# Two fp32 transformer layers on one core: the MLP's first norm between output projections, the last projection quarter inside the MLP, pinned row maxima, earlier V weights, another QKV order

## The chip, the cores and the metric

The kernel runs on one core of one Trainium2 chip. Its time is the device time of one execution in microseconds (us); three runs were shown before the change. The profile is one execution recorded by the hardware profiler. Engines are called as the profile calls them: PE is TensorE (matmuls), DVE is VectorE, ACT is ScalarE, POOL is GpSimd, and SP issues DMAs. ACT and POOL issue DMAs too.

## The reference

Two layers, with the same weights in both, on x of shape (1, 2048, 512) in fp32:

```python
def _A_ref(x, wqkv, wo):
    B, S, D = x.shape
    H = 32
    Dh = D // H
    qkv = (lambda x, *d: x.transpose(*d))((x @ wqkv).reshape(B, S, 3, H, Dh), 2, 0, 3, 1, 4)
    q, k, v = qkv[0], qkv[1], qkv[2]
    scores = jnp.einsum("bhqd,bhkd->bhqk", q, k) * (Dh ** -0.5)
    p = _softmax(scores, axis=-1)
    o = jnp.einsum("bhqk,bhkd->bhqd", p, v)
    return (lambda x, *d: x.transpose(*d))(o, 0, 2, 1, 3).reshape(B, S, D) @ wo

def _B_ref(x, w1, b1, w2):
    h = jnp.einsum("bsd,df->bsf", x, w1) + b1
    sp = jnp.log1p(jnp.exp(-jnp.abs(h))) + jnp.where(h > 0, h, jnp.zeros_like(h))
    act = h * jnp.tanh(sp)
    return jnp.einsum("bsf,fd->bsd", act, w2)

x = x + _A_ref(_layernorm(x, axis=-1), A_wqkv, A_wo)
x = x + _B_ref(_layernorm(x, axis=-1), B_w1, B_b1, B_w2)
# and both lines once more
```

D is 512, there are 32 heads of 16, 2,048 positions, and the MLP is 1,792 wide.

## The kernel before

**Number format.** A value x that a projection multiplies is kept as two parts, hi = x rounded by a copy to the matmul's format and lo = x - hi. `mm3` (L158) multiplies hi by hi, hi by lo and lo by hi: three matmuls of 128x512 for one product. `split_psum` (L154) makes the two parts of a result: ACT copies hi, DVE subtracts lo. In names, `th`/`tl`, `oh`/`ol`, `ah`/`al` are such pairs.

**Tiles.** The positions are worked in four chunks of 512 (`c`). Large tiles (8 KB a partition) come from one pool `blk` of 22 buffers; `tmp` holds small ones: `raw` (three buffers, shared by the blocks `pt` on their way to memory and by weights before they are split), `f` (two, shared by the activation `hb`, the normalised rows `xn` and the attention output `ot`), `he` and `hr` (one each, shared with the reciprocals `den`). The matmul results live in banks `s` (three), `mx` (two pairs) and `acc` (one).

**Norm.** `norm_parts` (L165) takes the statistics of four row blocks (L176, L177), the inverse root on POOL (L173), scales (`xn`, L188), transposes on PE (`tp`, L196) and splits (L197). It is a generator: every `yield` is a place where a caller goes on with something else.

**QKV.** `qkv` goes through a written list `order` of pairs (m, c): m is a block of 128 columns (0 to 3 queries, 4 to 7 keys), c the chunk. Each takes 12 matmuls, is split into `pt` and stored to memory (`scr`) on ACT's DMA queue (L466). When all chunks of m = 0 and m = 4 are through, `prep_qk(0)` (L236) loads the rows of the first four heads back, and the blocks that follow have some row maxima between them (`some_max`, L289 on PE and L293 on DVE). The V weights `rqkv4`, `rqkv5` are fetched after (5, 3) on ACT's DMA queue and split at once by ACT (L114) and POOL (L115). In layer 0 the split weights are stored (`keep`, L103) and in layer 1 read back (`ready`). The norm of the last chunk in layer 1 (`late`) is called when the list first asks for that chunk.

**Attention.** `run` makes 512 steps per layer of scores (L343, L353), exponentials on ACT (L344, L354) and the product with V (`pv`, L369), and beside them the maxima of the blocks 24 steps ahead. A block's maxima become the negative rows `nf` (ACT, L315) and `np` (POOL, L316 and L317), which SP's DMAs put into the query rows. Work is hung on steps by `hooks`. PE's order is chained by `pe` (L225).

**Output.** `HeadsOut` (L512) loads a chunk's sums and denominators (`num`, `den`), inverts (L529), spreads the reciprocals through memory (`rscr` L531, `rec` L537, both on POOL's queue), multiplies (L541) and splits (L545 to L548). The four numbers at L688 say at which steps from the end this is done for chunks 0 to 2; chunk 3 is done after the loop. `wo_parts` (L551) is the projection of a chunk, 48 matmuls, with the residual added on DVE (L567). Projection 0 fills the end of the attention loop, then come projection 1, the whole norm of chunk 0 for the MLP (L712), projection 2, projection 3.

**MLP.** `hid` (L572) makes one 128-wide step `f` of 14: 12 matmuls, then a chain over ACT (L582, L584, L586, L587), DVE (L583, L585, L590, L592) and POOL (L588, L591) to `ah` and `al`. `outp` (L595) multiplies them into four banks, two steps later (`LAG`). The norms of the next chunks are hung on steps with `spread` (L204).

**Order.** A scheduler orders the instructions of each engine by a simulated time line, except where `tc.keep_in_program_order` pins one to its written place.

Of the kernel before, what the change touches and what calls it, by code (L numbers as in the profile page):

```python
# [18 lines left out]
P = 128  # L19
# [22 lines left out]
FILL = 13  # L42
# [4 lines left out]
MAX_M = (2, 6, 3, 7)  # L47
# [5 lines left out]
def kernel(ctx: ExitStack, tc: tile.TileContext, x, wqkv, wo, w1, b1, w2, out):  # L53
# [45 lines left out]
    kept = {}  # L99
# [5 lines left out]
    def split_load(key, src, a, b, later=None, behind=False):  # L105
        t = b8([P, 2, a, b], F32R, "s" + key)
        raw = tmp.tile([P, a, b], F32, tag="raw", name="r" + key, bufs=3)
        if behind:
            tc.keep_in_program_order(nc.scalar.dma_start(raw, src))
        else:  # L110
            nc.sync.dma_start(raw, src)

        def split():
            nc.scalar.activation(t[:, 0], raw, AF.Copy)  # L114
# [25 lines left out]
    def ready(key, l, behind=False):  # L140
        t = b8(list(kept[key].shape), F32R, f"{key}l{l}")
        if behind:
            tc.keep_in_program_order(nc.scalar.dma_start(t.bitcast(F32), kept[key].bitcast(F32)))
        else:
            nc.sync.dma_start(t.bitcast(F32), kept[key].bitcast(F32))
        return t
# [7 lines left out]
    def split_psum(hi, lo, src):  # L154
        nc.scalar.activation(hi, src, AF.Copy)  # L155
        nc.vector.tensor_tensor(lo, src, hi.bitcast(F32), op=ALU.subtract)
# [8 lines left out]
    def norm_parts(src, nm, got, key, tag, fine=False):  # L165
        st = tmp.tile([P, NCH, 6], F32, tag="st", name=f"st{nm}")
        mv = tmp.tile([P, NCH, 2], F32, tag="mv", name=f"mv{nm}")
        ve = tmp.tile([P, NCH], F32, tag="ve", name=f"ve{nm}")
        rs = tmp.tile([P, NCH], F32, tag="rs", name=f"rs{nm}")

        def rstd(t, n):
            nc.vector.tensor_scalar(ve[:, t : t + n], mv[:, t : t + n, 1], EPS, None, op0=ALU.add)
            nc.gpsimd.tensor_tensor(rs[:, t : t + n], ve[:, t : t + n], mhalf[:, t : t + n], op=ALU.pow)  # L173

        for t in range(NCH):
            nc.vector.bn_stats(st[:, t], src[:, t])  # L176
            nc.vector.bn_aggr(mv[:, t], st[:, t])  # L177
            if fine:
                rstd(t, 1)
        if not fine:  # L180
            rstd(0, NCH)
        yield
        th = b8([P, KT, CW], F32R, f"th{nm}")
        tl = b8([P, KT, CW], F32R, f"tl{nm}")
        got[key] = (th, tl)
        for t in range(NCH):
            xn = t512("f", f"xn{nm}{t}")
            nc.vector.tensor_scalar(  # L188
                xn, src[:, t], mv[:, t, 0:1], rs[:, t : t + 1], op0=ALU.subtract, op1=ALU.mult
            )  # L190
            if tag == "mx":
                tp = ps.tile([P, 2, 512], F32, tag=tag, name=f"tp{nm}{t}")[:, 0]
            else:
                tp = pbank(tag, f"tp{nm}{t}")
            for k in range(KT):
                nc.tensor.transpose(tp[:, ts(k, P)], xn[:, ts(k, P)], ident)  # L196
            split_psum(th[:, :, ts(t, P)], tl[:, :, ts(t, P)], tp.rearrange("p (k n) -> p k n", k=KT))  # L197
            yield
# [5 lines left out]
    def spread(hooks, at, src, nm, got, key):  # L204
        parts = norm_parts(src, nm, got, key, "acc")
        for c, f in at:
            hooks.setdefault((c, f), []).append(lambda: next(parts, None))

    class Attention:
# [26 lines left out]
        def prep_qk(self, g):  # L236
            l = self.l
            ks, qs = [], []
            for u in range(HG // 2):
                k = b8([P, S], F32R, f"ks{l}{g}{u}")  # L240
                q = b8([P, S], F32R, f"qs{l}{g}{u}")
                m, h0 = divmod(g * HG + 2 * u, P // DH)
                for e in range(2):
                    r0 = e * HALF
                    nc.sync.dma_start(
                        k[r0 + KROWS : r0 + MROWS].bitcast(F32).rearrange("p (r n) -> p r n", n=P),
                        ones[:, None, :].to_broadcast([MROWS - KROWS, S // P, P]),
                    )
                    yield
                    for t, parts, base in ((k, K_PARTS, NCH), (q, Q_PARTS, 0)):  # L250
                        for j, a in enumerate(parts):
                            nc.sync.dma_start(
                                t[r0 + j * DH : r0 + (j + 1) * DH].bitcast(F32),
                                self.scr[base + m][a, (h0 + e) * DH : (h0 + e + 1) * DH, :].bitcast(F32),
                            )
# [51 lines left out]
        def max_rows(self, b, nm):  # L307
# [8 lines left out]
            nc.gpsimd.tensor_copy(np_[:, 0], nf)  # L316
            nc.gpsimd.tensor_tensor(np_[:, 1], nf, np_[:, 0].bitcast(F32), op=ALU.subtract)  # L317
# [111 lines left out]
    def load_qkv(l, wts, which, behind=False, later=None):  # L429
        for j in which:  # L430
            key = f"qkv{j}"
            if l:
                wts[j] = ready(key, l, behind)
            elif j < 4:
                wts[j] = split_load(key, *cols(wqkv, j), behind=behind, later=later)
            else:
                wts[j] = split_load(key, *rows2(wqkv[:, 2 * D : 3 * D], j - 4), behind=behind)

    def qkv(l, wts, tt, order, late):
# [4 lines left out]
        def some_max():  # L444
            if ahead[0] < AHEAD + PRE:
                att.chained = True
# [6 lines left out]
        for m, c in order:  # L453
# [15 lines left out]
            if (m, c) == (5, 3) and 4 not in wts:  # L469
                load_qkv(l, wts, (4, 5), behind=True)  # L470
            if m in (0, 4):
                done += 1
                if done == 2 * NCH:
                    for _ in att.prep_qk(0):
                        pass
            elif done == 2 * NCH and m in MAX_M:
                some_max()
        for c in range(NCH - 1):
            for i, _ in enumerate(v_parts(l, c, wts, tt, att, False)):
                if i % KT == KT - 1:  # L480
# [31 lines left out]
    class HeadsOut:  # L512
# [15 lines left out]
        def invert(self):  # L528
            tc.keep_in_program_order(nc.vector.reciprocal(self.den, self.den))  # L529
            for q in range(NCH):  # L530
                nc.gpsimd.dma_start(self.rscr[:, ts(q, P)], self.den[ts(q, H)])  # L531

        def spread(self):
            self.rec = b8([P, KT, CW], F32, f"rec{self.l}{self.c}")
            rows = self.rscr.rearrange("(k h) n -> k h n", k=KT)
            for h in range(P // DH):
                nc.gpsimd.dma_start(self.rec[ts(h, DH)], rows[:, h][None].to_broadcast([DH, KT, CW]))  # L537

        def parts(self, aside):
            nm = f"{self.l}{self.c}"  # L540
            tc.keep_in_program_order(nc.vector.tensor_tensor(self.num, self.num, self.rec, op=ALU.mult))  # L541
# [6 lines left out]
            nc.vector.tensor_tensor(ol, self.num, oh.bitcast(F32), op=ALU.subtract)  # L548
            self.out = oh, ol

    def wo_parts(l, c, outs, wot, x2, pe):  # L551
        oh, ol = outs[c].out
        for t in range(NCH):
            if t % 2 == 0:
                acc = ps.tile([P, 2, 512], F32, tag="mx", name=f"wo{l}{c}{t}")
            for k in range(KT):
                mm3(
                    acc[:, t % 2],
# [6 lines left out]
            if t % 2:  # L565
                x2v = x2[:, t - 1 : t + 1]
                nc.vector.tensor_tensor(x2v, acc, x2v, op=ALU.add)  # L567
# [68 lines left out]
    splits = []  # L636
    xc = [load_x(0)]
    load_qkv(0, wts, (0, 2), later=splits)
    xc.append(load_x(1))
    for c in range(NCH):  # L640
        parts = norm_parts(xc[c], f"q0{c}", tt, c, "mx", c == 0)
        next(parts)
        if c == 0:
            for split in splits:
                split()
        for _ in parts:
            pass
        if c == 0:
            load_qkv(0, wts, (1, 3))
        if c + 2 < NCH:  # L650
            xc.append(load_x(c + 2))
    for l in range(2):
        if l == 0:
# [4 lines left out]
        att = qkv(l, wts, tt, order, late)  # L658
# [29 lines left out]
        for c, (t0, t1, t2, t3) in enumerate(((-42, -23, -21, -18), (-26, -22, -20, -13), (-10, -6, -4, 0))):  # L688
# [14 lines left out]
        for i in range(1, 3):  # L703
            load_w1(i)
            load_w2(i - 1)
        for _ in fill:
            pass
        for i, _ in enumerate(project(1)):
            if i == 2 * KT:
                outs[3].invert()  # L710
                outs[3].spread()
        norm(x2s[0], f"m{l}0", tts, 0, "acc")  # L712
        for i, _ in enumerate(project(2)):
            if i == 2 * KT:
                outs[3].parts(False)
        for _ in project(3):
            pass
        for i in range(3, 7):
            load_w1(i)
            load_w2(i - 1)  # L720
        load_w2(6)
        hooks = {}
        for c in range(NCH - 1):
            spread(hooks, [(c, f) for f in range(5, 10)], x2s[c + 1], f"m{l}{c + 1}", tts, c + 1)
        wts, tt = {}, {}
        if l == 0:
            last = NCH - 1
            for f, js in ((2, (0,)), (4, (2,)), (9, (1,)), (11, (3,)), (12, (4,)), (13, (5,))):
                hooks.setdefault((last, f), []).append(lambda js=js: load_qkv(1, wts, js, behind=True))
# [34 lines left out]
```

## Time and profile before

| what | us |
|---|---|
| median of three runs | 3669.9 |
| the three runs | 3669.79, 3669.9, 3671.78 |
| the profiled execution: its own time | 3673.71 |
| its span | 3671.9 |
| its mean granted TensorE clock | 0.988 |
| TensorE busy | 3572.7 (97%) |
| VectorE busy | 2962.8 (81%) |
| ScalarE busy | 2522.5 (69%) |
| POOL busy | 556.0 (15%) |
| DVE reduces of the row maxima (L293) | 2388.5 |

The stages in the profiled execution: QKV of layer 0 to about 191, its attention to 1472, projections and MLP to 1864; QKV of layer 1 from 1839 to 2018, its attention to 3302, projections and MLP to the end. A busy share is a mean over stages with different limits; what a change is worth is read from the waits of the stage it touches. In an answer of the trace, square brackets give the idle time of the engine before an instruction and what ended it. `PEclk` is the clock that was granted to TensorE, 1.00 being full.

### The profile page before, as it was taken

Reading aid. Unit: us, or ns where it says so; the run is one execution under the profiler, and the core shown is the slowest. Engines: PE = TensorE matmul, PEld = TensorE weight load, DVE = VectorE, ACT = ScalarE, POOL = GpSimd, SP = SyncE. Lnnn points to the kernel's source line nnn. Section 1 sums busy time; section 2 is a strip of 40 time slices with the busy share of each in tenths; the row PEclk is TensorE's granted clock in tenths of the full one; section 3 lists DMA queues with packets and bytes.
Section 4 is the critical chain, followed back from the end, with each engine's and each line's share of the span. In section 5 each row is a group of like instructions: output and inputs, shape, how many; then the busy total and the mean of one; then the engine's idle time right before and its main releaser. Section 6 shows DMA issues by size and latency. Waiting matters only on the chain. (4 is left out here: it accounts for less than half of the span.)

```text
span 3671.9 us, 69455 instructions
## 1 busy us (share of the span) xinstructions
PE 3572.7 (97%) x28784; PEld 1957.3 (53%) x28784; DVE 2962.8 (81%) x2974; ACT 2522.5 (69%) x3475; POOL 556.0 (15%) x561
## 2 busy tenths in 40 slices
PE   7999999999999999899989999999999999999998
PEld 5644444444444444687766444444444444447887
DVE  5679999999999993566647799999999999936565
ACT  2178888888888887244421788888888888862444
POOL 2200101010010002344420000000000000023544
PEclk9999999999999999999999999999999999999999
DMA  7541322313121124600154311112021220246000
GB/s 240 199 105 37 79 52 73 62 36 80 45 72 46 43 77 68 199 12 12 46 181 155 72 31 34 36 39 43 19 45 30 44 45 31 68 68 196 12 12 24
DMA packets 128651, 254.07 MB, mean 69 GB/s; under 512 B 18512, under 2 KB 62544, under 8 KB 114512
## 3 DMA queue, kind: packets, MB, share of 16 engines
q1 hardware_dynamic: 102256, 176.75, 19.7%
q10 hardware_dynamic: 18816, 40.90, 3.1%
q0 software_dynamic: 7264, 31.99, 3.1%
q8 instruction: 226, 3.70, 0.4%
q14 instruction: 89, 0.73, 0.1%
HBM read 148.38 MB, written 99.09 MB: 67 GB/s over the span
## 5 line engine op out<-in xcount | busy, mean ns | idle before, releaser
L293 DVE TENSOR_REDUCE mxv<-pm 128x2 f32<-128x1024 f32 x2048 | 2388.5, 1220 | 192.8 <-PE pm L289 147.1
L344 ACT ACTIVATE p<-sp 128x1024 f32<-128x1024 f32 x1366 | 1396.7, 1022 | 25.0 <-PE sp L343 16.6
L369 PE MATMUL pv<-p,va 128*32 128x128 f32 (+3 forms) x16048 | 1174.1, 394 | 0.0
L289 PE MATMUL pm<-ks,qs 48*128 48x512 f32 x4096 | 1107.1, 446 | 5.3 <-DVE mxv L293 3.5
L354 ACT ACTIVATE p<-ss 128x512 f32<-128x512 f32 x1364 | 815.8, 598 | 393.3 <-PE ss L353 275.3
L343 PE MATMUL sp<-qs,ks 50*128 50x512 f32 x2732 | 743.8, 448 | 8.6 <-ACT p L344 6.1
L289 PEld LDWEIGHTS pm<-ks,qs 48*128 48x128 f32 x4096 | 460.6, 184 | 367.1 <-issue 226.5
L369 PEld LDWEIGHTS pv<-p,va 128*32 128x32 f32 x16048 | 369.4, 109 | 500.3 <-issue 419.9
L353 PE MATMUL ss<-qs,ks 50*128 50x512 f32 x1364 | 613.9, 450 | 0.2
L353 PEld LDWEIGHTS ss<-qs,ks 50*128 50x128 f32 x1364 | 252.7, 185 | 309.3 <-ACT p L354 206.5
L343 PEld LDWEIGHTS sp<-qs,ks 50*128 50x128 f32 x2732 | 280.0, 184 | 207.1 <-ACT p L344 118.6
L316 POOL CAST np<-nf 16x128 fp32r<-16x128 f32 x64 | 17.9, 280 | 2266.2 <-ACT nf L315 2266.2
L588 POOL TENSOR_TENSOR hb<-hb,he 128x512 f32<-128x512 f32 x112 | 157.3, 1404 | 225.1 <-DVE he L585 216.2
L586 ACT ACTIVATE hr<-he 128x512 f32<-128x512 f32 x112 | 70.9, 633 | 161.2 <-POOL hb L591 80.5
L592 DVE TENSOR_TENSOR al<-hb,ah 128x512 fp32r<-128x512 f32 x112 | 109.0, 974 | 88.2 <-POOL hb L591 86.8
L591 POOL TENSOR_TENSOR hb<-hb,hr 128x512 f32<-128x512 f32 x112 | 159.8, 1427 | 131.9 <-DVE ah L590 116.2
L155 ACT ACTIVATE pt<-qk 128x512 fp32r<-128x512 f32 x64 | 37.7, 597 | 167.7 <-PE qk L163 116.7
L584 ACT ACTIVATE he<-he 128x512 f32<-128x512 f32 x112 | 70.8, 632 | 98.9 <-DVE he L583 95.8
L590 DVE TENSOR_TENSOR ah<-hb,hr 128x512 fp32r<-128x512 f32 x112 | 78.1, 697 | 64.1 <-ACT hr L587 40.9
L585 DVE SCALAR_TENSOR_TENSOR he<-he 128x512 f32<-128x512 f32 x112 | 80.0, 715 | 40.7 <-ACT he L584 38.0
L582 ACT ACTIVATE hb<-h,b1t 128x512 f32<-128x512 f32 x112 | 76.5, 685 | 43.0 <-DVE al L592 33.0
L583 DVE TENSOR_SCALAR he<-hb 128x512 f32<-128x512 f32 x112 | 67.2, 600 | 46.5 <-POOL hb L588 33.1
(219 smaller groups left out, 3275.1 us busy)
## 6 DMA issues: line engine op xcount, KB each, us to landing
scr<-pt ACTq DMA_DIRECT2D x64, 512.0 KB
qs<-scr SPq DMA_DIRECT2D x192, 128.0 KB
ks<-scr SPq DMA_DIRECT2D x192, 128.0 KB
vscr<-v SPq DMA_DIRECT2D x32, 512.0 KB
va<-vscr SPq DMA_DIRECT2D x64, 256.0 KB
oscr<-ot SPq DMA_DIRECT2D x64, 256.0 KB
ww<-sw POOLq DMA_DIRECT2D x14, 1024.0 KB, 5.1
qs<-np SPq DMA_DIRECT2D x512, 2.0 KB
```

Of the source, the lines that this page charges most:

```text
L289: nc.tensor.matmul(pm[:, e], qs[u][rows, q0 : q0 + P], ks[u][rows, ts(n, 512)], start=True, stop=True)
L293: nc.vector.tensor_reduce(self.mxs[b][:, 2 * u : 2 * u + 2, qt, n], pm, axis=AX.X, op=ALU.max)
L343: self.pe(nc.tensor.matmul(sp[:, e], k, q, start=True, stop=True))
L344: nc.scalar.activation(self.pts[-1][:, 0:n], sp[:, 0:n], AF.Exp, scale=SCALE)
L353: self.pe(nc.tensor.matmul(sp, k, q, start=True, stop=True))
L354: nc.scalar.activation(self.pts[i // 3][:, 2], sp, AF.Exp, scale=SCALE)
L369: nc.tensor.matmul(self.accs[b][ts(h, VW), cols], self.va[b // NCH][:, kt, h, :], self.pts[j][:, e, cols], start=kt == 0 and q0 == 0, stop ...
L585: nc.vector.scalar_tensor_tensor(e, e, 2.0, e, op0=ALU.add, op1=ALU.mult)
L588: nc.gpsimd.tensor_tensor(hb, hb, e, op=ALU.mult)
L590: nc.vector.tensor_tensor(ah, hb, r, op=ALU.mult)
L591: nc.gpsimd.tensor_tensor(hb, hb, r, op=ALU.mult)
L592: nc.vector.tensor_tensor(al, hb, ah.bitcast(F32), op=ALU.subtract)
```

## The change

Ten things change, most of them the place at which an instruction is written or whether it is pinned there.

1. The V weights get a tile of their own (`rawv`), are fetched on SP's queue after block (1, 2), and are split after block (2, 0); the stores of split weights are collected and issued after block (6, 0).
2. Half of the row loads of the first four heads go through POOL's DMA queue.
3. Other QKV orders in both layers. Maxima come with m = 6, 3, 7 instead of 2, 6, 3, 7, and every third product in V's blocks instead of every fourth. PE's order is chained from `prep_qk(0)` on.
4. `np`, the stores and loads of the reciprocals, and the subtraction `ol` are pinned to their written place.
5. The steps at which chunks 0 and 1 are inverted, spread and multiplied change; projection 0 starts to fill one step later (`FILL`).
6. The MLP norm of chunk 0 is written in pieces between the blocks of projections 1 and 2, pinned, on the banks `s`.
7. Chunk 3 is inverted and spread during projection 2 instead of projection 1.
8. Projection 3 is written inside the MLP, a quarter at each of the steps 5 to 8, on the bank `acc`; chunk 3's multiply is at step 2.
9. Most of the MLP's weight loads move to steps 0 to 9 of the MLP.
10. The norms in the MLP are pinned on VectorE; the one of chunk 1 is at steps 8 to 12 instead of 5 to 9.

```diff
-FILL = 13
+FILL = 12
-MAX_M = (2, 6, 3, 7)
+MAX_M = (6, 3, 7)
...
-    def split_load(key, src, a, b, later=None, behind=False):
+    def split_load(key, src, a, b, later, raw=None):
         t = b8([P, 2, a, b], F32R, "s" + key)
-        raw = tmp.tile([P, a, b], F32, tag="raw", name="r" + key, bufs=3)
-        if behind:
-            tc.keep_in_program_order(nc.scalar.dma_start(raw, src))
-        else:
-            nc.sync.dma_start(raw, src)
+        if raw is None:
+            raw = tmp.tile([P, a, b], F32, tag="raw", name="r" + key, bufs=3)
+        nc.sync.dma_start(raw, src)
 
         def split():
             nc.scalar.activation(t[:, 0], raw, AF.Copy)
             nc.gpsimd.tensor_tensor(t[:, 1], raw, t[:, 0].bitcast(F32), op=ALU.subtract)
-            keep(key, t)
-
-        if later is None:
-            split()
-        else:
-            later.append(split)
+            unkept.append((key, t))
+
+        later.append(split)
...
+    def behind(ins):
+        return tc.keep_in_program_order(ins)
+
+    def norm_parts(src, nm, got, key, tag, fine=False, pin=lambda ins: ins, pe=lambda ins: ins, halves=False):
...
-            nc.vector.tensor_scalar(
-                xn, src[:, t], mv[:, t, 0:1], rs[:, t : t + 1], op0=ALU.subtract, op1=ALU.mult
+            pin(
+                nc.vector.tensor_scalar(
+                    xn, src[:, t], mv[:, t, 0:1], rs[:, t : t + 1], op0=ALU.subtract, op1=ALU.mult
+                )
             )
+            if halves:
+                yield
...
-        parts = norm_parts(src, nm, got, key, "acc")
+        parts = norm_parts(src, nm, got, key, "acc", pin=behind)
...
-                    nc.sync.dma_start(
+                    queue = nc.gpsimd if g == 0 and e else nc.sync
+                    queue.dma_start(
...
-            nc.gpsimd.tensor_copy(np_[:, 0], nf)
-            nc.gpsimd.tensor_tensor(np_[:, 1], nf, np_[:, 0].bitcast(F32), op=ALU.subtract)
+            behind(nc.gpsimd.tensor_copy(np_[:, 0], nf))
+            behind(nc.gpsimd.tensor_tensor(np_[:, 1], nf, np_[:, 0].bitcast(F32), op=ALU.subtract))
...
-            if (m, c) == (5, 3) and 4 not in wts:
-                load_qkv(l, wts, (4, 5), behind=True)
+            for fn in due.get((m, c), []):
+                fn()
             if m in (0, 4):
                 done += 1
                 if done == 2 * NCH:
                     for _ in att.prep_qk(0):
                         pass
+                    att.chained = True
...
-            order = [(0, 0), (4, 0), (0, 1), (4, 1), (1, 0), (0, 2), (4, 2), (1, 1), (0, 3), (4, 3)]
+            order = [(0, 0), (4, 0), (1, 0), (5, 0), (0, 1), (4, 1), (1, 1), (0, 2), (4, 2), (0, 3), (4, 3)]
+            due[1, 2] = [lambda: load_qkv(0, wts, (4, 5), splits)]
+            due[2, 0] = [split_all]
+            due[6, 0] = [keep_all]
         else:
-            order = [(0, 0), (0, 1), (0, 2), (4, 0), (4, 1), (4, 2), (1, 0), (0, 3), (4, 3)]
+            order = [(0, 0), (0, 1), (0, 2), (4, 0), (4, 1), (4, 2), (1, 0), (1, 1), (1, 2), (5, 0), (0, 3), (4, 3)]
...
-        for c, (t0, t1, t2, t3) in enumerate(((-42, -23, -21, -18), (-26, -22, -20, -13), (-10, -6, -4, 0))):
+        for c, (t0, t1, t2, t3) in enumerate(((-42, -20, -19, -13), (-26, -19, -18, -11), (-10, -6, -4, 0))):
...
-        for i in range(1, 3):
-            load_w1(i)
-            load_w2(i - 1)
+        load_w1(1)
+        load_w2(0)
         for _ in fill:
             pass
+        first = norm_parts(x2s[0], f"m{l}0", tts, 0, "s", pin=behind, pe=att.pe, halves=True)
         for i, _ in enumerate(project(1)):
-            if i == 2 * KT:
+            for n in range({0: 1, 6: 1, 9: 2, 12: 2, 15: 2}.get(i, 0)):
+                next(first)
+        for i, _ in enumerate(project(2)):
+            if i == 1:
+                next(first)
+            if i == 3:
                 outs[3].invert()
                 outs[3].spread()
-        norm(x2s[0], f"m{l}0", tts, 0, "acc")
-        for i, _ in enumerate(project(2)):
-            if i == 2 * KT:
-                outs[3].parts(False)
-        for _ in project(3):
-            pass
-        for i in range(3, 7):
-            load_w1(i)
-            load_w2(i - 1)
-        load_w2(6)
+        load_w1(2)
+        load_w2(1)
         hooks = {}
+
+        def on(f, fn, c=0):
+            hooks.setdefault((c, f), []).append(fn)
+
+        on(2, lambda: outs[3].parts(False))
+        rest = wo_parts(l, 3, outs, wot, x2s[3], lambda ins: ins, False)
+
+        def quarter():
+            for _ in range(KT):
+                next(rest)
+
+        for f in range(5, 9):
+            on(f, quarter)
+        on(9, lambda: next(rest, None))
+        for i, (f1, f2) in enumerate(((0, 0), (2, 2), (4, 6), (7, 8)), 3):
+            on(f1, lambda i=i: load_w1(i))
+            on(f2, lambda i=i: load_w2(i - 1))
+        on(9, lambda: load_w2(6))
         for c in range(NCH - 1):
-            spread(hooks, [(c, f) for f in range(5, 10)], x2s[c + 1], f"m{l}{c + 1}", tts, c + 1)
+            spread(hooks, [(c, f) for f in (range(8, 13) if c == 0 else range(5, 10))], x2s[c + 1], f"m{l}{c + 1}", tts, c + 1)
```

More of the change, by code (lines that the diff above doesn't have):

```diff
@@ L427, in run, with load_qkv @@
             open_banks()
-    def load_qkv(l, wts, which, behind=False, later=None):
+    def load_qkv(l, wts, which, later):
+        raw = None
         for j in which:
@@ L636, with split_all, keep_all @@
     splits = []
+    def split_all():
+        while splits:
+            splits.pop(0)()
+    def keep_all():
+        while unkept:
+            keep(*unkept.pop(0))
     xc = [load_x(0)]
-    load_qkv(0, wts, (0, 2), later=splits)
+    load_qkv(0, wts, (0, 2), splits)
     xc.append(load_x(1))
@@ L643 @@
         if c == 0:
[L644 to L645 removed]
+            split_all()
         for _ in parts:
```

76 lines of the change are left out of this document (42 added, 34 removed).

## The prediction

> **What bounds the kernel now.** I read the page's first part, then the waits, then TensorE's timeline around each wait, then stretches with their clock.
>
> ```profile
> span 3671.9 us, 69455 instructions
> ...
> PE 3572.7 (97%) x28784; PEld 1957.3 (53%) x28784; DVE 2962.8 (81%) x2974; ACT 2522.5 (69%) x3475; POOL 556.0 (15%) x561
> ```
>
> TensorE (PE) works 97% of the span. Almost everywhere a 128x512 matmul starts 0.227 us after the one before, so a block of 12 takes 2.72 us. Time can come only from its stalls.
>
> ```profile
> DVE num L541 <- DMA rec<-rscr: 44.8, 5, 15.3
> ...
> ACT sqkv L114 <- DMA qs<-scr: 12.9, 1, 12.9
> ...
> PE tpm L196 <- DVE tlm L156: 12.5, 6, 3.3
> ...
> PE qk L161 <- DVE pt L156: 9.8, 3, 7.9
> ...
> PE tpq L196 <- DVE tlq L156: 7.6, 2, 4.7
> ...
> PE sp L343 <- ACT p L344: 6.1, 15, 3.9
> ```
>
> The columns are total us, times, longest. Placed on TensorE's timeline (start, duration, and in brackets the idle time before and its releaser):
>
> ```profile
> 98.64 0.80 PE L161 MATMUL qk<-thq,sqkv 128*128 128x512 f32 x1 [7.88 <-DVE pt L156]
> ...
> 1415.41 0.47 PE L343 MATMUL sp<-qs,ks 50*128 50x512 f32 x1 [0.89 <-DMA qs<-np]
> ...
> 1499.06 0.92 PE L196 MATMUL tpm<-ident,xnm 128*128 128x128 f32 x4 [3.32 <-DVE tlm L156]
> ...
> 1517.11 0.50 PE L161 MATMUL wo<-wo0l,oh 128*128 128x512 f32 x1 [2.50 <-ACT oh L547]
> ...
> 1880.05 1.94 PE L196 MATMUL tpq<-ident,xnq 128*128 128x128 f32 x8 [4.66 <-DVE tlq L156]
> ...
> 3244.80 0.86 PE L343 MATMUL sp<-qs,ks 50*128 50x512 f32 x2 [3.92 <-ACT p L344]
> ```
>
> A stall costs more than its length: the clock then falls. The stretches below list the busy time of each engine, the granted clock, the DMA share and GB/s. After the 0.89 us stall TensorE ran at half rate from 1417.3 to 1431.0, after the 3.92 one for 17.1 us.
>
> ```profile
> 65.00:95.00 30.00, 24.18 (x106) 18.19 (x105) 11.72 (x13) 3.64 (x7) 0.00 (x0) 0.97 0.96 254
> ...
> 1400.00:1432.00 32.00, 30.35 (x217) 11.51 (x216) 9.17 (x4) 22.40 (x31) 15.29 (x26) 0.79 0.52 81
> ...
> 1490.00:1520.00 30.00, 20.55 (x79) 15.30 (x78) 13.62 (x19) 4.53 (x6) 5.12 (x9) 0.83 1.02 326
> ...
> 3236.00:3262.00 26.00, 22.09 (x140) 7.99 (x142) 9.17 (x4) 14.38 (x20) 6.86 (x8) 0.67 0.44 67
> ```
>
> The attention loops between the tails keep their built order on TensorE (4,672 rows alike in each layer) and on ScalarE (1,442), so I leave them at zero.
>
> **The change, part by part.** Gains are in us of the profiled execution, in brackets the low and high end.
>
> Start: the first key and query blocks wait 1.28 (to 44.34) for the norm's copies. With the new order the block after does not need the next chunk so soon: 1.3 (0 to 2.6).
>
> V weights: ScalarE waits 12.90 for a raw tile whose load was issued at 88.50, and everything behind it in ScalarE's queue (the copy of a finished block) waits too; TensorE loses 7.88, then 2.4 because 12 matmuls take 5.12 at the lower clock, and 1.6 at 82.85 on a late `ks`: 11.9 in all. Afterwards the load stands behind the first rows of queries and keys, in a tile of its own, and the first row maxima come ten blocks later. DMA is the limit: in 65 to 95 its share is 0.96, and the queue with the 24 row loads takes 48% of 30 us, 14.5; the eight or nine stores share the other 14.3, 1.6 each. Afterwards these loads, 1 MB of V (3.2 by the stores' rate) and nine stores (14.4) are 32.1 against ten blocks of cover, 27.2: 4.9 late. Three `pt` buffers take up two stores (3.2), 1.7 is left and as much again for the clock: I count 4 as staying. Gain 7.9 (2 to 11.9). The half of the loads moved to POOL's queue passes nothing but the V residuals and the deferred stores, which wait for nobody.
>
> L0 tail: POOL issued eight `rec` loads before the low half of `np` (written 1408.07), so the query rows came late. At the cadence of 1.675 per `pair` the 32 us lost 6.5. The two `np` instructions now stand before them: 6 (0 to 6.5). L1 tail: VectorE's `num` waited 15.31 for `rec`, ScalarE's next `p` waited 3.90 for the buffer, and slow matmuls followed: 9.4 lost. The loads and the multiply now stand six steps apart, not three (15 us at 2.5 a step, 512 steps in 1,281 us), and the `p` that takes over the buffer comes later. What is late next is the second multiply, two steps behind: I leave 0.5 of each tail, so 8.9 (3 to 9.4). The first projection's filling starts one step later (FILL), with the same matmuls: nothing.
>
> L0 projection to MLP: the norm's transposes wait 3.32, 1.52, 1.41, then 0.69 to the first `h` at 1505.80, less what transposes need anyway: 8.8. Thirty matmuls then take 8.81 instead of 6.81 (2.0); with 2.50 for `oh` and 1.1 for the residual add this makes 14.4. In the built order nine or more projection matmuls (2.0 us) lie between transposes, while 0.54 of scaling, 0.67 of `tlm` and 0.60 of `thm` are done, and 42 lie between the last transposes and the first `h`. I put the first `h` at about 1498. Row by row from there, the chain of the activation (0.68, 0.42, 0.63, 0.69, 0.63, 0.72, 0.69, 1.3, 0.69) gives the first `al` 10 us later, and TensorE has 58 matmuls (13.2) first. The multiply `num` and `ol` (2.29 each, with 1.92 of ScalarE between) now stand on VectorE ahead of the fourth `al`: all that is behind them, that `al` included, slips by about 6, of which TensorE sees 1.5 to 2. I count 2.5: gain 11.9 (5 to 14.4). The last quarter's reciprocal with its 4 stores and 8 `rec` loads moves from the second projection to the third, on POOL behind the norm's power. The first `he` takes over the reciprocal's buffer and so waits for the four stores, issued some 5 us before it: covered. The loads landed 11.7 us after issue in the median under a DMA share of 1.02; issued at about 1499 they land by 1511, the multiply stands at about 1517, and beyond 6 us of delay each us is one of TensorE's. L1 the same without the 2.50: 11.7 less 2.5, 9.2 (4 to 11.7). The weight loads moved behind the first `hid` steps are needed 8 us or more after issue; cover gone, one 1 MB load costs 3.
>
> Inside the MLP, norm instructions on VectorE keep their written place: four statistics (0.65 each), beside the 1.5 us in which VectorE waits for ScalarE's logarithm. I take a loss of 1 (loss 8 to gain 3: before, TensorE's longest wait on `al` was 1.0; four more of these, doubled by the clock, at worst).
>
> Seam to L1: before, 1.39, 4.66, 0.69 and 3.0 of slow matmuls, 9.7. Two things count against each other. Three more blocks (8.2) go ahead of the last chunk's norm. But the last two output steps now follow with nothing between, while the chain is the slower of the two: `al` comes every 6.55 us.
>
> ```profile
> 1800.00 0.68 DVE L592 TENSOR_TENSOR al<-hb,ah 128x512 fp32r<-128x512 f32 x1
> ...
> 1806.55 0.68 DVE L592 TENSOR_TENSOR al<-hb,ah 128x512 fp32r<-128x512 f32 x1
> ```
>
> On that clock TensorE waits 1.2 and 2.2 for the last two `al`, some 2 for the first late transpose (it came 11.7 after the last output matmul; cover is 8.2 plus transposes), and 1.5 of lower clock: 7 of the 9.7 return. Gain 2.5 (-3 to 9.7). L1 row loads: 2.89 and 0.63 at 1920 and 1.6 of lower clock; more blocks ahead of the first maxima: 3.5 (0 to 5.1).
>
> Sum: 1.3 + 7.9 + 6 + 11.9 - 1 + 2.5 + 3.5 + 8.9 + 9.2 = 50.2. The profiled execution took 3673.7 (span 3671.9), 3.8 above the median of the runs, 3669.9. 3673.7 - 50.2 = 3623.5, less 3.8: 3620.
>
> The clock of the stalls that stay is the softest part. By the row at 1415, 0.89 of waiting was followed by 13.7 us of half rate; yet 1.28 at 44.34 was followed by none.
>
> The Trainium skill (TensorE: Matmul & The Clock Gate, Part 1) says that the clock falls only after an idle window of some 3.4 us. The 0.89 us row disagrees, so the sum keeps the lower clock; by the rule the waits that stay would cost only themselves: without the 1.7 of V, the 1.5 of the seam and 1 of the MLPs, an estimate of 3616.
>
> **Rivals.**
>
> *The V stall returns.* For it: DMA share 0.96, and everything ScalarE does is behind the split. Against: nothing on TensorE needs keys until ten blocks later. If loads and V run one behind the other, it loses the full 11.9 and a little: 3620 + 9 = 3629.
>
> The Trainium skill (DMA: Bandwidth & Descriptors, Issuing engines are not separate DMA queues) says that a second issuing engine saves only issue time, as all share the same 16 engines. The 0.96 agrees; by it POOL's half of the loads makes them no sooner.
>
> *The activation chain takes over.* The waits on `al` and `num` in the first and last MLP chunks grow to 5 each with the clock behind them, four places: 3640. For it: 4.8 us of such waits already. Against: in 1560 to 1640 TensorE worked 79.98 of 80.
>
> *The tails only shift.* `num` is late for another `p`: both tails come back, 3635.
>
> *Slower.* One mechanism: the norm instructions kept in place on VectorE hold each hidden step of the MLP at the pitch of the steps with scaling between (7.16, `al` to `al`, 1732.55 to 1739.71) instead of the 5.89 that chunks 1 and 2 average: 1.27 x 84 steps (three chunks, two layers) = 107, 3727. It decides from 0.6 a step (50.2 / 84). Against: only five steps of 14 in a chunk hold such instructions, and before has the scaling there too.
>
> *No effect.* If stores and tails were bound by DMA alone, new orders would leave all waits: 3670.
>
> **How the numbers follow.** Forecast 0.60; V returns 0.13; chain 0.14; tails 0.05; slower 0.06; no effect 0.02. The lows add to 3 and the highs to 74, not all at once; the rivals up to 3640 are inside and the range goes to 3652 for two together; below, two thirds of what separates 50 from 74 gives 3603. About 0.2% (7 us) is what a measurement can tell: faster 0.92, same 0.02, slower 0.06.
>
> **What would show it.** No idle of 7 us before `qk` at 90 to 100 and ScalarE's wait for the raw V tile under 4; no half rate at 1417 and 3243 less the shift; first `h` less than 8 us after the last projection of chunk 2; waits on `al` near the fourth hidden step and at the end of the last chunk, under 3 each. Wrong if TensorE's wait for `al` sums over 15, or if the first maxima still wait for `ks`.

## The result, and the profile after

Twelve runs of the changed kernel have a median of 3667.8 us (3664.7 to 3669.1), twelve of the kernel before, taken beside them, 3674.5 (3669.6 to 3684.8). The ratio is 0.9977 with a 95% interval of 0.9967 to 0.9988: faster by 0.23%, some 7 to 8 us, where 50 were forecast and the range ended at 3652. The profiled execution has a span of 3667.2.

Every stall that the prediction quoted at the ends of the attention and ahead of the MLP is gone, and the clock there is full. These are stretches of the changed kernel with the columns of the prediction's table (busy time by engine, granted clock, DMA share, GB/s):

```profile
80.00:100.00 20.00, 12.52 (x43) 9.25 (x42) 2.77 (x4) 2.10 (x5) 1.94 (x4) 0.83 1.02 261
1400.00:1432.00 32.00, 31.20 (x259) 11.63 (x258) 7.29 (x6) 28.15 (x39) 14.73 (x27) 1.00 0.53 84
1480.00:1510.00 30.00, 29.44 (x136) 24.10 (x135) 12.59 (x18) 8.22 (x13) 12.05 (x16) 1.00 1.03 332
1786.00:1836.00 50.00, 42.79 (x187) 31.59 (x187) 27.56 (x50) 21.34 (x35) 17.99 (x15) 1.00 0.11 43
3236.00:3262.00 26.00, 25.37 (x215) 10.31 (x211) 7.98 (x4) 21.32 (x29) 12.14 (x19) 1.00 0.69 110
```

The second, third and fifth lines are the tails and the way into the MLP: clock 1.00 where it was 0.79, 0.83 (over 1490 to 1520) and 0.67. The first line is the V fetch: the clock is still 0.83, and DMA is full. The fourth is the middle of layer 0's last MLP chunk: TensorE works 42.8 of 50 us at full clock, so it waits. The waits say for what (total us, times, longest), first before, then the changed kernel:

```profile
ACT hb L582 <- DVE al L592: 33.0, 35, 3.7
...
ACT pt L155 <- DMA scr<-pt: 24.4, 10, 5.0
...
PE mo L163 <- DVE al L592: 4.8, 7, 1.0
...
PE mo L161 <- DVE ah L590: 1.5, 3, 0.7
```

```profile
ACT hb L594 <- DVE al L604: 117.0, 68, 6.0
...
ACT pt L150 <- DMA scr<-pt: 26.9, 6, 8.3
...
PE mo L158 <- DVE al L604: 21.0, 29, 1.5
...
PE qk L156 <- DVE pt L151: 14.0, 6, 4.5
...
PE mo L156 <- DVE ah L602: 11.2, 8, 2.8
```

ScalarE's wait to begin a hidden step (`hb`) until the step before it has made its `al` rose from 33 to 117 us, and TensorE's waits for `al` and `ah` from 6.3 (4.8 and 1.5) to 32.2. The prediction named a wait for `al` of over 15 in sum as a sign that it is wrong; it is 21.0.

Where the time went, by stage. The borders are first and last matmuls of the named tiles in the two profiled executions; the third column is the first experiment below.

| stage, us | before | changed | xn apart | gain forecast | gain measured |
|---|---|---|---|---|---|
| start to the first product with V | 207.0 | 209.4 | 206.9 | 9.2 | -2.4 |
| the two attention loops up to 95% of their products | 2384.3 | 2386.6 | 2385.9 | 0 | -2.3 |
| L0 last 5% of the products | 73.4 | 66.3 | 65.9 | 6 | 7.0 |
| L0 from there to the first `h` | 33.2 | 25.9 | 25.9 | 11.9 with the waits after `h` | 7.3 |
| L0 MLP and seam, to L1's first product | 528.0 | 538.6 | 508.1 | 5 | -10.6 |
| L1 last 5% | 76.2 | 66.6 | 66.2 | 8.9 | 9.6 |
| L1 to the first `h` | 33.3 | 27.1 | 27.2 | 9.2 | 6.2 |
| L1 MLP, and to the end | 336.5 | 346.7 | 331.5 | 0 | -10.2 |

The gains of 30 us at the tails and ahead of the MLPs came; the MLPs, the start and the loops gave nearly all of it back. The row of layer 0's MLP holds two things: up to the first QKV block of layer 1 it is 14.4 us longer, and from there to the first product 3.8 shorter.

Why `hb` waits can be seen in ScalarE's queue in the last chunk. First before (its `al`, at 1800.00 and 1806.55, stand in the prediction), then the changed kernel, then the changed kernel's `al` on VectorE:

```profile
1799.26 0.68 ACT L582 ACTIVATE hb<-h,b1t 128x512 f32<-128x512 f32 x1
...
1805.81 0.68 ACT L582 ACTIVATE hb<-h,b1t 128x512 f32<-128x512 f32 x1
```

```profile
1794.46 0.69 ACT L594 ACTIVATE hb<-h,b1t 128x512 f32<-128x512 f32 x1 [2.92 <-DVE al L604]
...
1801.88 0.69 ACT L594 ACTIVATE hb<-h,b1t 128x512 f32<-128x512 f32 x1 [2.92 <-DVE al L604]
```

```profile
1793.73 0.69 DVE L604 TENSOR_TENSOR al<-hb,ah 128x512 fp32r<-128x512 f32 x1 [1.40 <-POOL hb L603]
1794.34 0.54 DVE L187 TENSOR_SCALAR xnq<-x,mvq,rsq 128x512 f32<-128x512 f32 x1
```

Before, `hb` of the next step starts at 1799.26, ahead of the `al` at 1800.00: two steps overlap. In the changed kernel it starts at 1794.46, just after `al` has ended (1794.42), after 2.92 us of idling, and the pitch is 7.42 instead of 6.55. The cause lies in two buffers, called `f`, that `hb` and `xn` share. The trace gives no buffer numbers; these starts fit one reading, and experiments 1 to 4 put it to the test. In before the scheduler let `hb` of the next step take the buffer of the last `xn`, free as soon as its transposes were read, and `xn` waited for `al`. Pinned, `xn` comes first and takes the last `xn`'s buffer; what is left for `hb` is the buffer of the `hb` before it, which `al` is the last to read.

### The profile page after: what moved, and what is told of

The parts are those of the page before. It is cut to its first block, busy times and chain, and to the rows that moved or that the text cites. A ratio compares the mean times of both kernels' runs of the same rounds, so it can differ in the third digit from the quotient of the medians.

```text
span 3667.2 us, 69407 instructions
## 1 busy us (share of the span) xinstructions
PE 3568.3 (97%) x28784; PEld 1950.0 (53%) x28784; DVE 2968.4 (81%) x2978; ACT 2522.6 (69%) x3475; POOL 567.0 (15%) x589
```

## The experiments

**1. xn in buffers of its own.** On the changed kernel:

```diff
-            xn = t512("f", f"xn{nm}{t}")
+            if tag == "acc":
+                xn = tmp.tile([P, 2, 512], F32, tag="raw", name=f"xn{nm}{t}", bufs=3)[:, 0]
+            else:
+                xn = t512("f", f"xn{nm}{t}")
```

> The changed kernel, but the normalised rows xn that are made inside the MLP lie in the three buffers called raw (idle there) and no longer in the two that they share with the activation hb; pins and orders stay. Theory A (buffers): pinned in place, xn takes the buffer of the xn before it, and hb of the next hidden step is left with the buffer of the step just before, so ScalarE must wait for that step's al; the pitch of al in the last chunk of layer 0 was 7.4 us where it was 6.55 before. With buffers of its own the pitch falls under 6.6, the MLPs lose the 12 us each that they gave back, the seam some 3 more: 25 us (18 to 32) less than the changed kernel, about 3642. Theory B (VectorE has too much to do in order: the pinned statistics, num and ol stand ahead of al): the pitch stays above 7 where they stand, and the time within 6 us of the changed kernel's.

3619.5 us (3619.1 to 3621.4); ratio to before 0.9851 (0.9836 to 0.9866). That is 48 us under the changed kernel with every pin in place (the pins hold not VectorE's instructions alone, but also ScalarE's copy `hi` of each transposed block): theory A, and twice its size. The waits:

```profile
ACT hb L597 <- PE h L158: 60.3, 40, 11.7
...
ACT hb L597 <- DVE al L607: 18.1, 22, 2.7
...
PE mo L158 <- DVE al L607: 3.4, 5, 1.1
```

ScalarE now waits for TensorE (`h`), as it should where TensorE is the bound, and TensorE's waits for `al` fell from 21.0 to 3.4. The last `al` of layer 0 comes at 1821 instead of 1863. The size was wrong in part because the sharing had slowed before too (33.0 above); experiment 4 puts that part at 12 to 15 us.

**2. The pins off.** On the changed kernel:

```diff
-        parts = norm_parts(src, nm, got, key, "acc", pin=behind)
+        parts = norm_parts(src, nm, got, key, "acc")
```

> The changed kernel with the norms inside the MLP no longer pinned on VectorE; all else as changed. Theory A: the scheduler again writes hb of the next step before xn, xn waits for al instead of hb, the pitch goes back to some 6.55 in the last chunk: 14 us (8 to 22) less than the changed kernel, about 3653. Theory B agrees on a gain here, since the pinned statistics go with the pins. A third (projection 3's quarter and the multiply of chunk 3 inside the MLP cost the 12 us): within 4 us of the changed kernel.

3633.1 us (3628.9 to 3636.4), 35 under the changed kernel, more than the 8 to 22 expected; `hb` waits 51.9 for `al`, TensorE 7.2, and the pitch in the last chunk is again 6.55. With experiment 1 this rules out that VectorE simply had too much to do in order: there the pins stay and the time falls further.

**3. The pins alone, on before.** The scaling, statistics and splits of `spread`'s norms are pinned, nothing else:

```diff
-        parts = norm_parts(src, nm, got, key, "acc")
+        parts = norm_parts(src, nm, got, key, "acc", tc.keep_in_program_order)
...
-            nc.vector.tensor_scalar(
+            pin(
+                nc.vector.tensor_scalar(
```

> The kernel before with one edit: the norms inside the MLP (statistics, scaling and both halves of the split) pinned to their written place, xn still in the two buffers it shares with hb. Theory A (the pin swaps the buffers, and hb of the next step waits for al): the pins alone cost it about what taking them off gave the changed kernel, 25 to 38 us more than before, about 3706; pitch of al in the last chunk of layer 0 above 7.2 and ScalarE waiting 2.9 for al before hb. Rival (the loss needs projection 3 and the multiply inside the MLP as well): under 8 us more than before.

3694.6 us (3692.4 to 3698.5) against 3674.0: ratio 1.0058 (1.0039 to 1.0078), 20.6 us slower. The pitch in the last chunk is 7.41, as in the changed kernel, and the waits are its waits:

```profile
ACT hb L584 <- DVE al L594: 106.2, 62, 6.0
...
PE mo L163 <- DVE al L594: 22.6, 30, 1.5
```

So neither the last projection quarter nor the multiply inside the MLP is needed for the loss. The size is below the 25 expected.

**4. Buffers apart, on before.** The same edit as in 1, on the kernel before, for the norms inside the MLP alone.

> The kernel before with one edit: the xn of the norms inside the MLP in the three raw buffers, as in the first experiment; no pins, nothing else of the change. Theory A says what the change is worth once the buffers are apart: the difference between this kernel and the first experiment, which the prediction's sum put at 50. Before already waited 33 us in all for al ahead of hb and had the 6.55 pitch over ten steps of layer 0's last chunk, so I expect 5 to 15 us less than before here, about 3664, and 45 between the two. Rival (the buffers alone make most of the first experiment's gain, the other parts of the change little): 25 us or more less than before, 3649 or under.

3656.8 us (3651.6 to 3658.6) against 3668.7: ratio 0.9960 (0.9946 to 0.9974), 12 to 15 us. Between this kernel and experiment 1 lie 37 us by the medians, 40 by the two ratios: that is what the rest of the change is worth where the buffers don't collide, in place of 50.

**5. The tails alone, on before.** Beside what is shown, the stores and loads of the reciprocals, `ol` and the residual adds are pinned, as in the changed kernel:

```diff
-FILL = 13
+FILL = 12
...
-            nc.gpsimd.tensor_copy(np_[:, 0], nf)
-            nc.gpsimd.tensor_tensor(np_[:, 1], nf, np_[:, 0].bitcast(F32), op=ALU.subtract)
+            tc.keep_in_program_order(nc.gpsimd.tensor_copy(np_[:, 0], nf))
+            tc.keep_in_program_order(nc.gpsimd.tensor_tensor(np_[:, 1], nf, np_[:, 0].bitcast(F32), op=ALU.subtract))
...
-        for c, (t0, t1, t2, t3) in enumerate(((-42, -23, -21, -18), (-26, -22, -20, -13), (-10, -6, -4, 0))):
+        for c, (t0, t1, t2, t3) in enumerate(((-42, -20, -19, -13), (-26, -19, -18, -11), (-10, -6, -4, 0))):
```

> The kernel before with the attention tails of the change alone: np, the stores and loads of reciprocals, the multiplies' second half and the residual adds pinned, the new steps, and FILL at 12. Theory: the tails' gains stand for themselves, 7.0 us in layer 0 and 9.6 in layer 1 by the milestones: 16 us (12 to 19) less than before, no half clock at 1417 or 3243. Rival: the gain needs the new order after the loop; then under 8 us.

3658.5 us (3655.6 to 3660.0) against 3675.0: ratio 0.9954 (0.9937 to 0.9970), 16.5 less, as expected. The clock is whole in both tails:

```profile
1400.00:1432.00 32.00, 30.95 (x270) 11.93 (x264) 8.05 (x7) 28.23 (x38) 14.73 (x27) 1.00 0.53 85
3236.00:3262.00 26.00, 24.97 (x197) 10.20 (x200) 10.03 (x5) 19.63 (x27) 9.85 (x14) 1.00 0.63 97
```

**6. The old QKV stage in the changed kernel.** Orders, V fetch, queues and maxima of before in both layers:

```diff
-MAX_M = (6, 3, 7)
+MAX_M = (2, 6, 3, 7)
...
-                    queue = nc.gpsimd if g == 0 and e else nc.sync
+                    queue = nc.sync
...
-            due[1, 2] = [lambda: load_qkv(0, wts, (4, 5), splits)]
-            due[2, 0] = [split_all]
-            due[6, 0] = [keep_all]
+            due[5, 3] = [lambda: load_qkv(0, wts, (4, 5), splits)]
```

> The changed kernel with the QKV stage of before in both layers: the old orders, V weights fetched on ScalarE's queue through the raw buffers after block (5, 3), all first row loads on SP, maxima with m = 2 too. Theory: the new front gave nothing, since the stores wait for the same saturated DMA engines: the first product with V comes 2.4 us sooner than in the changed kernel (at 207), layer 1's at about the same distance from the MLP's end; the time is 1 to 5 us less, 3664. Rival: the new orders did gain the 11.9 of the old V wait and something else at the start took it away; then this one is 8 us or more slower, 3676.

3672.3 us (3668.7 to 3678.6), ratio 0.9997 (0.9987 to 1.0006): more than the changed kernel by 4.4 by the medians, by 7 by the two ratios; neither what was expected nor what the rival said. In its profile L0's first product with V is at 210.5, only 1.1 later than in the changed kernel, and L1's 6.6 later; but the profiled execution is the slowest of its ten, so its stages don't place the difference. The new stage is worth some 4 to 7 us in both layers together, not the 12.7 of the forecast (9.2 and 3.5).

Experiments 7 to 12 differ from experiment 1 by 2 to 7 us in their medians, and the 95% intervals of all their ratios overlap with its own. Their waits, each read from one execution, say more than their times.

**7. The stores of split weights really deferred.** The changed kernel writes them after block (6, 0), but does not pin them, and POOL still issued four of 1 MB from 15 us on. On experiment 1:

```diff
-            keep(*unkept.pop(0))
+            keep(*unkept.pop(0), behind)
```

> The changed kernel with xn in buffers of its own (the first experiment, 3619.5), and the stores of the split QKV weights of layer 0 pinned where they are written, after block (6, 0): in the changed kernel the scheduler still issued the first four (1 MB each) before 25 us. Theory C (the start is bound by DMA: stores of blocks wait behind those 4 MB): TensorE's wait for the second chunk's transposes at 36 us falls from 2.8 to 5.9 to under 1.5, time 3 to 6 us less than the first experiment. Rival (the wait there is that of the loads of x or of VectorE's order): no change, within 2 us.

3621.3 us (3618.1 to 3626.6): no gain. The wait at 36 us is gone, as theory C said, and half the QKV blocks are done 3.3 us sooner than in experiment 1; but the six stores, now issued together between 106.4 and 109.1, bring the wait back in another place, on ScalarE:

```profile
119.77 0.60 ACT L150 ACTIVATE pt<-qk 128x512 fp32r<-128x512 f32 x1 [7.81 <-DMA scr<-pt]
...
125.65 0.60 ACT L150 ACTIVATE pt<-qk 128x512 fp32r<-128x512 f32 x1 [5.28 <-DMA scr<-pt]
```

and in the stretch around it:

```profile
115.00:130.00 15.00, 11.71 (x41) 7.77 (x41) 7.17 (x8) 1.79 (x3) 0.73 (x1) 0.77 0.96 391
```

DMA 0.96, 391 GB/s, clock 0.77. A block's `pt` buffer is free only when its store has landed. The first product with V comes 9.1 later than in experiment 1, in the slowest of the four runs.

**8. The stores written one by one between the V products.** On experiment 1, with `due[6, 0]` taken out:

```diff
                 if i % 3 == 0:
                     some_max()
+                if i % 8 == 0 and unkept:
+                    keep(*unkept.pop(0), behind)
```

> The first experiment with the six stores of split QKV weights pinned one by one between the V products of layer 0 (every eighth product, 145 to 190 us) and none before. Theory C (block stores wait on saturated DMA engines, and the g1 kernel only moved the 6 MB into the next full stretch, where it lost 12 us between 78 and 143): the wait of 3 to 6 at 36 us is gone as there, and no wait over 1 us comes at 115 to 140; time 3 to 7 us less than the first experiment, about 3615. Rival (the delayed stores hold ScalarE or POOL wherever they are put): as slow as g1_keep or slower, 3621 or more.

3616.2 us (3615.1 to 3617.2), ratio 0.9840 (0.9826 to 0.9855): 3.3 under experiment 1, inside the expected 3 to 7, and of the kernels tried the fastest along with number 12. But the stores are not where the expectation has them, at 145 to 190. The pin keeps their order on POOL alone, and POOL, which had only V tiles to clear between them, issued five of them at 98.9, 101.3, 107.7, 110.0 and 112.3 and the sixth at 163.6. So what differs from experiment 7 is that five stores are spread over 13 us in place of six over 3, and that they begin sooner. From 98 to 115 DMA is as full as there (0.96, 387 GB/s) and ScalarE waits for `scr<-pt`, but 5.09 and 3.97 where it was 7.81 and 5.28, and TensorE has no wait in these 17 us. The wait at 36 us is gone as in experiment 7. The first product with V is at 202.1, and 115 to 130 is quiet:

```profile
115.00:130.00 15.00, 15.00 (x68) 10.36 (x67) 11.73 (x13) 2.39 (x4) 0.00 (x0) 1.00 0.56 223
```

**9. V fetched sooner still.** On experiment 1:

```diff
-            due[1, 2] = [lambda: load_qkv(0, wts, (4, 5), splits)]
+            due[0, 1] = [lambda: load_qkv(0, wts, (4, 5), splits)]
```

> The first experiment with the raw V weights fetched after block (0, 1) instead of (1, 2), when the DMA share is under a half. Theory C (the waits at 83 to 97 are block stores that queue behind row loads and V on saturated DMA engines): 1 MB less in that window, 2.5 us of its DMA time; the two waits there together fall from 7.2 to about 4.5, time 2 to 4 us less than the first experiment. Rival (the row loads alone hold the stores, V comes behind them): within 1.5 us.

3622.4 us (3621.1 to 3625.6), 2.9 more. The two waits are 3.86 and 3.50, together 7.4 against 7.2. V is not what the blocks wait for: the rival's reason, that the row loads alone hold the stores, fits the waits, though not its 1.5 us; experiment 10 bears it out.

**10. All row loads on SP.** On experiment 1:

```diff
-                    queue = nc.gpsimd if g == 0 and e else nc.sync
+                    queue = nc.sync
```

> The first experiment with all row loads of the first four heads on SP's queue again. Theory C: the 16 DMA engines are the limit, not the issuing queue, so the two waits at 83 to 97 stay between 6 and 9 together and the time is within 2 us. Rival (two issuing queues make the rows come sooner): 3 us or more slower than the first experiment.

3626.6 us (3619.9 to 3630.0), 7.1 more by the medians, with one run as fast as experiment 1; the profile is of the slowest. Theory C is wrong by its own sign. The two waits at 83 to 97 don't stay: they are 1.24 and 1.66, together 2.9 in place of 7.2. SP alone issued the 24 row loads from 72.6 to 95, SP and POOL together in experiment 1 from 71.1 to 84.7, so with two queues more loads stood beside the stores of the blocks. Of these 4 us only 1.6 reach the first product with V, since TensorE now waits 3.03 at 103.8 for VectorE's maxima. The Trainium skill (DMA: Bandwidth & Descriptors, Issuing engines are not separate DMA queues) says that a second issuing engine saves only the time of issuing, which is usually small, since all run on the same 16 engines; here the issuing of these loads took some 9 us longer on one queue, so it was not small.

The loss is in layer 1, whose QKV stage takes 9.8 more, and for 4 us of it the profile has the place, on VectorE in the norm of the last chunk; first this kernel, then experiment 1:

```profile
1832.61 5.98 DVE L190 TENSOR_SCALAR xnq<-x,mvq,rsq 128x512 f32<-128x512 f32 x2
```

```profile
1833.54 0.54 DVE L190 TENSOR_SCALAR xnq<-x,mvq,rsq 128x512 f32<-128x512 f32 x1
```

Of the two, the first takes 5.53. POOL clears three V tiles there (5.33, from 1832.53). In experiment 1 the first of its row loads stood ahead of them in its queue and kept them away until 1873.

**11. Two more blocks ahead of the late norm.** On experiment 1:

```diff
-(1, 0), (1, 1), (1, 2), (5, 0), (0, 3), (4, 3)]
+(1, 0), (1, 1), (1, 2), (5, 0), (5, 1), (5, 2), (0, 3), (4, 3)]
```

> The first experiment with two more QKV blocks, (5, 1) and (5, 2), ahead of the last chunk's norm in layer 1. With the activation chain no longer the bound, TensorE there waits 3.7, 1.5, 0.5 and 0.6 for that norm; two blocks are 5.4 us of cover. If nothing else binds: 4 us less than the first experiment, about 3615. Rival: fewer blocks are left between the row loads and the first maxima, and the wait at 1890 (2.6) grows by as much: within 2 us.

3623.9 us (3614.7 to 3626.4): not faster, and the profile is of the slowest run. The wait of 3.69 for the norm is still there at 1831.6, so the scheduler did not use the two blocks as cover for its first transposes, and the row maxima now wait 2.21 for `ks` and 2.79 for VectorE.

**12. Both.** Experiments 8 and 11 together.

> Both edits, the stores between the V products and the two blocks ahead of the late norm, on the first experiment. If the two are independent, the sum of their differences: about 3611 by theory C; by both rivals 3621.

3616.3 us (3616.0 to 3617.9): experiment 8's time, neither the 3611 nor the 3621 expected. The two don't add: what 11 lost alone does not show here. With 11's scatter of 12 us, I take its loss as unsettled and its lack of gain as shown.

## Why the prediction was wrong

*Inside the MLP: "I take a loss of 1".* This step failed, and it carried most of the miss: 35 of the 48 us between 3620 and 3667.8 are gone once the pins are taken off (2). Layer 1's MLP by itself lost 10.2, more than the 8 that the step took as the worst for both. It asked which instructions the pins put on VectorE and how long they take. It did not ask which buffer they get. The pins swapped the buffers of `xn` and `hb`, and TensorE then waited for the chain in both MLPs, 32.2 us in place of 6.3: with the swap away (experiment 1) the time is 3619.5, with the pins alone (3) before loses 20.6. That the forecast of 3620 for the whole change is nearly the time of experiment 1 is chance: 12 of it come from what ailed before as well (4).

*Seam: 2.5.* The step took before's 6.55 pitch for the chain's own and worked out waits of 1.2 and 2.2 for the last two `al`. For the last two steps TensorE waited 1.13 for `ah` and 0.90 for `al`, then 2.24 for `ah` and 0.45 for `al`; but nine more waits for `al` of 0.65 to 1.5 lay ahead of them in the chunk, since the pitch had become 7.4. The wait for the late norm did go: 4.66 before, 1.01 at 1893 now.

*V weights and start: 7.9 and 1.3.* Gain -2.4 in the profile. The V wait did go, and the stall came back as 2.98 and 4.50 with the clock at 0.83: the rival "the V stall returns", though not for V (9). The step let 4 us stay, and 7.5 of waiting stayed, with slow matmuls behind them. Its sum counted the DMA work in total, not which store stands behind which loads; with the loads on one queue the two waits are 2.9 (10), so the second queue, which the step took as harmless, is part of it. ScalarE's waits for stores show where the blocks stood, here and at the start:

```profile
34.23 0.60 ACT L150 ACTIVATE pt<-qk 128x512 fp32r<-128x512 f32 x1 [6.27 <-DMA scr<-pt]
...
95.69 0.60 ACT L150 ACTIVATE pt<-qk 128x512 fp32r<-128x512 f32 x1 [8.26 <-DMA scr<-pt]
```

The total for `scr<-pt` says little: it is 26.9 against 24.4 before. At the start the step counted no DMA at all: the block order (1, 0), (5, 0) put two stores more beside 4 MB of weight stores, the fourth block waited 6.27 for a buffer at 34.23, the copies of the second chunk's norm stood behind it, and TensorE waited 5.89 at 36.75. Experiments 7 and 8, without weight stores there, have no such wait. That the two block stores are needed for it is not tested alone; in the kernel before, with the weight stores as early and the old order, TensorE waits 2.37 at 28.35, for VectorE.

*L1 row loads: 3.5.* The 2.89 and 0.63 went, and 1.69 and 1.80 on finished blocks came in their place, at 1922 and 1927.

*The tails: 6 and 8.9.* Right: 7.0 and 9.6 by the stages, 16.5 on their own (5).

*Projection to MLP: 11.9 and 9.2.* The order did what the step said: it worked out the first `h` of layer 0 7.8 sooner (1498 for 1505.80), and the stage gave 7.3; in layer 1 it gave 6.2. What the step added for waits after the first `h` falls into the MLP, where it can't be told from the loss. The wait near the fourth hidden step is 0.39 at 1537.6, less than the 1.5 to 2 expected.

*The slower rival* had the right place and nearly the right pitch (7.16 against 7.42 measured), but not the buffers as its reason. Against it the prediction held that only five steps of 14 in a chunk hold such instructions. That is so for the first three chunks of both layers; layer 0's last chunk has them in thirteen, layer 1's in none. *The activation chain takes over* named what TensorE would wait for: not 5 us in each of four places, as it had it, but 37 waits of at most 2.8 over both MLPs.

*The clock.* The sum let waits that stay cost slow matmuls too. In 1786 to 1836 nine waits of 0.45 to 0.91 left the clock at 1.00; but behind 2.75 at 1582.47 it is 0.58 (1584 to 1588), and behind 2.24 at 1860.57 it is 0.53 (1861 to 1863). The Trainium skill's rule (TensorE: Matmul & The Clock Gate, Part 1) that the clock falls after an idle window of some 3.4 us agrees with the nine, and disagrees with these two and with the 0.89 us at 1415 in before.

## What to carry to other kernels

Pinning an instruction that allocates from a rotating pool also pins who gets which buffer; before costing a pin by its engine time, list for each tile of the pool whose last reader frees it, in the built order of both kernels. A stage that is bound by full DMA engines gained nothing here from a fetch that was moved within it (9). Spreading bytes looks better: six stores issued within 3 us brought TensorE's waits back in another place (7), five spread over 13 us did not (8), though these began 7.5 us sooner as well, and no run tells the two apart. A pin holds an instruction's order on its own engine, not its time: read from the trace when it ran.

## What was not expected of the hardware

VectorE's scaling of 128x512 takes 0.54 us, but not while POOL clears V tiles (5.33 for three, back to back). In experiment 10 one scaling begins at 1832.61, 0.08 after the first clear does, and takes 5.53: it ends 0.28 after the last clear. In before one takes 3.19 and ends 0.27 after the last clear, and the traces of experiments 4, 5 and 6 have one each (1.84, 3.19 and 1.55) that ends 0.27 to 0.29 after it. So the scaling waits out all the clears that are left, not one of them. A subtraction of another tile (`pt`) beside the same clears in before takes its usual 0.69. The Trainium skill (SBUF — State Buffer, SBUF: two separate sides) says that POOL and some instructions of VectorE share a pair of ports, that whichever starts first has it for its whole instruction, and that the other is blocked; the five durations agree with that, and no run here separates it from other causes.
